# The first FFN product of six blocks by Strassen's algorithm in a fused attention and FFN kernel

## The chip, the cores and the metric

The kernel runs on one core of a Trainium2 chip. The metric is the device time of one execution in microseconds (us), the median of several runs. Engines are named as the profile names them: PE (TensorE matmul), PEld (its weight loads), DVE (VectorE), ACT (ScalarE), POOL (GpSimd) and SP (SyncE, which here issues all DMAs). L12 is line 12 of the kernel's source.

## The reference

Attention without softmax over 8 batches, 8 heads, 576 tokens and head size 64 feeds a token mixing of rank 32 and an FFN of 512 to 2048 to 512. Everything is fp32.

```python
kv = np.einsum('bhsd,bhse->bhde', k, v)
out = np.einsum('bhsd,bhde->bhse', q, kv)
rms = np.sqrt(np.mean(out * out, axis=-1, keepdims=True) + 1e-06)
x = out / rms * g_norm          # heads side by side: (8, 576, 512)
xt = x.transpose(0, 2, 1)
h = xt @ U @ V
u = x + h.transpose(0, 2, 1)
ch = np.maximum(u @ w_ch1, 0.0) @ w_ch2
return u + ch
```

## The kernel before

The 8 x 576 = 4608 tokens form `NBLK` = 9 blocks of `BLK` = 512. Hidden size 2048 is cut into `NF` = 16 chunks f of 128, model size 512 into `ND` = 4 chunks d. Activations lie transposed, features on partitions. An fp32 value is kept as two fp32r halves, hi and lo, and one fp32 product is three fp32r matmuls: hi·hi, hi·lo and lo·hi. So one f of a block has 4 x 3 matmuls of 128x512 in `ffn1` (L372 to L374) and 4 x 3 in `ffn2` (L389). `relu` makes the split hidden chunk: `hh` on ACT (L381), `hl` on DVE (L382). The chunk h has one PSUM bank (`ps_h`), y has four (`ps_y`) in which all 16 f are accumulated, and other products share three (`pp`). In program order ffn1 of f stands ahead of ffn2 of f-1.

All weights stay on chip. They arrive as encoded 64-bit words (`raw`, two 512 KB DMAs for each f) and are decoded in block 0, two f ahead of their use: `decode` on ACT (L82) and DVE (L85, L86, L88, L90) into a `dec` tile of 128x1024, then `split`: ACT copies the hi part into `ws` (L95), POOL subtracts for the lo part (L96).

The tokens of the next batch are prepared beside the FFN. For each of four head pairs: `kv_step` (k^T v), `out_step`, `stats_step`, `mul_step` (RMS norm), `xsplit_step` (xh, xl), `turn_step` (a transpose on DVE, L293, and 16 small DMAs `ut<-xt`, L296), `t_step`, `t4_step` (rank 32) and `mix_step`, whose two adds (L366) complete the rows `ut32` of u; `split_cols` makes `uth` and `utl` from them (L329, L330). `prep_schedule` gives each step a position, two to each f; head pairs follow every `gap` positions (STEPS0 with gap 3 in block 0, STEPS with gap 6 later). `finish` adds u to y (DVE L400, POOL L401) in one of three `st` buffers and sends it out (L402).

The written order is only a start: the tile framework's list scheduler orders the instructions of each engine from its own timeline, and each engine then runs its list in order. All DMAs are in one list, SP's. Tiles of pools with one buffer (`xt`, `kv_sb`, `q_sb`, `tails`) or three (`st`) make a later writer wait for the last reader.

Of the kernel before, what the change touches and what calls it, by code (L numbers as in the profile page):

```python
# [47 lines left out]
def build(ctx: ExitStack, tc: tile.TileContext, kv_in, kvt0_in, kvt_in, q_in, uv_in, g_in, w_in, out):  # L48
# [327 lines left out]
    def relu(h, end=False):  # L376
        if end:
            hh, hl = [sc.tile([P, BLK], F32R, name=f"h{s}_end", tag=f"x{s}") for s in "hl"]
        else:
# [1 line left out]
        nc.scalar.activation(out=hh, in_=h, func=AF.Relu)  # L381
        nc.vector.scalar_tensor_tensor(out=hl, in0=h, scalar=0.0, in1=hh.bitcast(F32), op0=ALU.max, op1=ALU.subtract)  # L382
# [9 lines left out]
    def finish(y, j):  # L392
        uh, ul = ut.pop(j)
        for c, cols, acc in y:
            if j == NBLK - 1:
                o = ut32[c][:, S - BLK + cols.start:S - BLK + cols.stop]
                nc.vector.scalar_tensor_tensor(out=o, in0=o, scalar=g_sb, in1=acc, op0=ALU.mult, op1=ALU.add)
            else:
                o = st.tile([P, DM], F32, name="st")
                nc.vector.tensor_tensor(out=o, in0=acc, in1=uh[:, c, :].bitcast(F32), op=ALU.add)  # L400
                nc.gpsimd.tensor_tensor(out=o, in0=o, in1=ul[:, c, :].bitcast(F32), op=ALU.add)  # L401
            nc.sync.dma_start(out=out[j, c][:, cols], in_=o)  # L402

    def outputs(j):

        y = [(c, slice(0, BLK), ps_y.tile([P, BLK], F32, name="y")) for c in range(ND)]
        if j == NBLK - 1:
            c, _, acc = y.pop()
            y.append((c, slice(0, BLK // 2), acc[:, 0:BLK // 2]))
            y.append((c, slice(BLK // 2, BLK), ps_p.tile([P, BLK], F32, name="pp")[:, 0:BLK // 2]))  # L410
        return y
# [80 lines left out]
    def prep_schedule(b):  # L492

        todo = {}
        if 0 < b <= B:
            todo[1] = [lambda: [split_cols(b - 1, c, 1, nc.gpsimd) for c in range(ND)]]
        if b < B:
            for p in range(NPAIR):
                steps = STEPS0 if b == 1 else STEPS
                base = steps["gap"] * p  # L500

                def kv(p=p):
                    kv_step(b, p)
                    nxt = (b, p + 1) if p + 1 < NPAIR else (b + 1, 0)
                    if nxt[0] < B:
                        load_kv(*nxt)

                def o(p=p):
                    for what in (out_step, stats_step, mul_step, xsplit_step, turn_step):
                        what(b, p)  # L510
                    nxt = (b, p + 1) if p + 1 < NPAIR else (b + 1, 0)
                    if nxt[0] < B:
                        load_q(*nxt)

                def t(p=p):
                    t_step(b, p)
                    t4_step(b, p)
# [95 lines left out]
```

## Time and profile before

| | |
|---|---|
| median of 3 runs | 941.3 us (940.36 to 941.7) |
| profiled execution | 941.2 us; span 939.4 us |
| busy: PE, DVE, ACT, POOL | 913.4, 428.2, 237.6, 88.7 us |
| first ffn1 of block 0; first ffn1 of block 1 | 39.46 us; 159.8 us |
| first ffn1 of block 8 | 848.1 us |
| DMA over the span | 65.48 MB, mean 70 GB/s |

Busy times are sums over the span. Since stages have different limits, a stage is read from its own stretch: how much of it each engine was busy, and which wait ended last. The clock column gives the TensorE clock that was granted, 1.00 for full speed. A matmul's "mean ns" in the groups counts overlapping neighbours twice; the spacing in the chain of work is its cost.

### The profile page before, as it was taken

What the parts mean: (1) busy time and instruction counts of PE and PEld (TensorE: products, weight loads), DVE (VectorE), ACT (ScalarE), POOL (GpSimd) and SP (SyncE); (2) the same over time, 40 slices, a digit from 0 to 9 for tenths busy, and PEclk for the clock granted to TensorE, in tenths of its full rate; (3) what the DMA queues carried; (4) which work ended last, traced back from release to release, by engine and by line L of the source; (5) the groups of instructions that cost most, each with busy time, mean ns of one, the idle gap of its engine ahead of it and who ended that gap; (6) DMA issues with size and microseconds to landing.
All of it is one profiled execution on the core that took longest, in us unless ns stands there. A gap on an engine that the chain in (4) does not pass through costs nothing.

```text
span 939.4 us, 11992 instructions
## 1 busy us (share of the span) xinstructions
PE 913.4 (97%) x4550; PEld 763.3 (81%) x4550; DVE 428.2 (46%) x824; ACT 237.6 (25%) x483; POOL 88.7 (9%) x82
## 2 busy tenths in 40 slices
...
DMA packets 45034, 65.48 MB, mean 70 GB/s; under 512 B 9904, under 2 KB 28080, under 8 KB 44976
## 3 DMA queue, kind: packets, MB, share of 16 engines
...
q14 instruction: 22, 0.18, 0.1%
...
## 4 chain that ended last, share of the span: by engine, by line
PE 84%; DVE 13%; DMA 1%; issue 1%; SPq 0%; ACT 0%; POOL 0%; DVEq 0%; POOLq 0%
PE y L389 37%; PE h L372 13%; PE h L373 13%; PE h L374 13%; DVE dec L88 3%; PE pp L219 2%; PE pp L240 2%; DVE dec L90 2%; DVE dec L86 2%; PE pp L304 2%; DVE dec L85 1%; DVE hl L382 1%; DMA w1raw<-w_in 1%; PE pp L364 1%; PE pp L389 1%
## 5 line engine op out<-in xcount | busy, mean ns | idle before, releaser
L389 PE MATMUL y<-hh,ws 128*128 128x512 f32 (+1 forms) x1072 | 351.0, 394 | 0.1
L382 DVE SCALAR_TENSOR_TENSOR hl<-h,hh 128x512 fp32r<-128x512 f32 x142 | 97.8, 689 | 307.8 <-ACT hh L381 307.2
L389 PEld LDWEIGHTS y<-hh,ws 128*128 128x128 f32 x1072 | 194.3, 188 | 36.0 <-ACT hh L381 0.8
L372 PE MATMUL h<-uth,ws 128*128 128x512 f32 x536 | 212.5, 397 | 6.9 <-DVE hl L382 6.9
L373 PE MATMUL h<-utl,ws 128*128 128x512 f32 x536 | 210.1, 392 | 0.0
L374 PE MATMUL h<-uth,ws 128*128 128x512 f32 x536 | 209.9, 392 | 0.0
L389 PE MATMUL y<-hl,ws 128*128 128x512 f32 (+1 forms) x536 | 207.6, 387 | 0.0
L381 ACT ACTIVATE hh<-h 128x512 fp32r<-128x512 f32 x142 | 84.8, 597 | 409.2 <-PE h L374 409.1
L372 PEld LDWEIGHTS h<-uth,ws 128*128 128x128 f32 x536 | 101.4, 189 | 31.0 <-DVE hl L382 10.8
L374 PEld LDWEIGHTS h<-uth,ws 128*128 128x128 f32 x536 | 101.2, 189 | 21.9
L373 PEld LDWEIGHTS h<-utl,ws 128*128 128x128 f32 x536 | 101.4, 189 | 20.4
L389 PEld LDWEIGHTS y<-hl,ws 128*128 128x128 f32 x536 | 100.6, 188 | 20.5
L401 POOL TENSOR_TENSOR st<-st,utl 128x512 f32<-128x512 f32 x32 | 40.7, 1296 | 676.7 <-DVE st L400 673.6
L366 DVE TENSOR_TENSOR ut<-pp,ut 128x288 f32<-128x288 f32 x56 | 25.0, 456 | 53.6 <-DMA ut<-xt 39.0
L96 POOL TENSOR_TENSOR ws<-dec,ws 128x1024 fp32r<-128x1024 f32 x15 | 37.4, 2495 | 60.6 <-ACT ws L95 60.6
L400 DVE TENSOR_TENSOR st<-y,uth 128x512 f32<-128x512 f32 x32 | 21.2, 686 | 44.5 <-PE y L389 33.0
L329 ACT ACTIVATE uth<-ut,g_sb 128x448 fp32r<-128x448 f32 (+7 forms) x56 | 27.6, 530 | 48.0 <-DVE ut L366 33.6
L330 DVE SCALAR_TENSOR_TENSOR utl<-ut,g_sb,uth 128x448 fp32r<-128x448 f32 (+7 forms) x56 | 28.2, 534 | 14.7 <-ACT uth L329 10.9
L253 DVE TENSOR_REDUCE ss<-x 128x10 f32<-128x640 f32 x32 | 26.1, 814 | 19.0 <-ACT x L244 19.0
L219 PE MATMUL pp<-kv_sb 128*128 128x128 f32 x232 | 31.4, 275 | 0.5 <-DVE t L313 0.5
L219 PEld LDWEIGHTS pp<-kv_sb 128*128 128x128 f32 x232 | 29.3, 191 | 2.0 <-DVE t L313 0.9
L240 PE MATMUL pp<-kvb,q_sb 128*128 128x128 f32 x224 | 29.6, 274 | 0.0
...
## 6 DMA issues: line engine op xcount, KB each, us to landing
raw<-w_in SPq DMA_DIRECT2D x30, 512.0 KB, 10.2
kv_sb<-kv_in SPq DMA_DIRECT2D x29, 512.0 KB, 3.5
...
out<-st SPq DMA_DIRECT2D x32, 256.0 KB, 2.0
ut<-xt SPq DMA_DIRECT2D x224, 20.0 KB, 1.8
ut<-xt SPq DMA_DIRECT2D x224, 16.0 KB, 1.8
...
kvq<-kv_in SPq DMA_DIRECT2D x3, 512.0 KB, 7.7
```

Of the source, the lines that this page charges most:

```text
L88: nc.vector.scalar_tensor_tensor(out=bits, in0=high, scalar=0xC0000000, in1=bits, op0=ALU.bitwise_and, op1=ALU.bitwise_or)
L96: lo_eng.tensor_tensor(out=lo, in0=src, in1=hi.bitcast(F32), op=ALU.subtract)
L219: nc.tensor.matmul(pp[:, 0:P], lhsT=m[:, i * P:(i + 1) * P], rhs=m[:, MAIN + i * P:MAIN + (i + 1) * P], start=(i == 0 and b < NATIVE), sto ...
L240: nc.tensor.matmul(big[:, i * P:(i + 1) * P], lhsT=qt[:, TAIL + i * P:TAIL + (i + 1) * P], rhs=kb, start=True, stop=True)
L330: nc.vector.scalar_tensor_tensor(out=lo, in0=src, scalar=g_sb, in1=hi.bitcast(F32), op0=ALU.mult, op1=ALU.subtract)
L372: nc.tensor.matmul(h, lhsT=w1s[f][0][:, d, :], rhs=uh[:, d, :], start=(d == 0), stop=False)
L373: nc.tensor.matmul(h, lhsT=w1s[f][0][:, d, :], rhs=ul[:, d, :], start=False, stop=False)
L374: nc.tensor.matmul(h, lhsT=w1s[f][1][:, d, :], rhs=uh[:, d, :], start=False, stop=(d == ND - 1))
L381: nc.scalar.activation(out=hh, in_=h, func=AF.Relu)
L382: nc.vector.scalar_tensor_tensor(out=hl, in0=h, scalar=0.0, in1=hh.bitcast(F32), op0=ALU.max, op1=ALU.subtract)
L389: nc.tensor.matmul(acc, lhsT=w2s[f][w][:, c, :], rhs=h[:, cols], start=(f == 0 and w == 0 and h is hh), stop=(f == NF - 1 and w == 1))
L401: nc.gpsimd.tensor_tensor(out=o, in0=o, in1=ul[:, c, :].bitcast(F32), op=ALU.add)
```

## The change

Blocks 0 to 2 stay as they are. Blocks 3 to 8 are taken in three pairs. A pair's u (512 x 1024 tokens) and w1 are cut in halves both ways: d halves by block halves for u (B11, B12, B21, B22), f halves (n and n + 8) by d halves for w1 (A11 to A22). Winograd's form of Strassen's algorithm computes the four quarters of h from 7 products in place of 8. Each product is of a weight form (`FORMS`) with a form of u (`WITH`), each again split in hi and lo: 2 x 3 = 6 matmuls of 128x512 (L517).

- The weight forms: A11, A12 and A22 are parts of w1, S1 to S4 sums of parts. `forms_of_w(n)`, eight times, positions in block 1, makes S1 to S4 on DVE (two L217 of 128x512, four L223 and four L228 of 128x256) and ACT (L224) in `st` buffers, and copies all seven (256 KB each) and the w2 of two f (512 KB each) to DRAM (L204): 22.9 MB.
- For each pair 8 x 7 forms are read back into a ring of 8 buffers, 7 loads ahead (L502); the w2 of a group, four tiles of 512 KB, is read into one set of buffers (L509).
- `forms_of_u` makes the seven forms of u for a pair, twice (two chunks i): 7 casts on ACT (L474), 7 subtractions (L475) and 4 more (L479) on DVE, all 128x512. u of blocks 3 to 8 is kept as one fp32 tile `r` (named `uth` or `utl` in the profile) in place of `uth`, `utl`.
- A pair runs in 4 groups of two row pairs: 14 products, with sums and relus between them (`after`; adds L524, `hl` L445), then 8 y units (`y_unit`, L565), each 12 matmuls in one bank of `ps_y`. After a unit DVE adds the bank to r (L524), or in the last group to an `st` tile that goes out.
- The lo part of a weight is subtracted on DVE (L105) in place of POOL, in block 0 also that of u's columns; `relu`'s special ending goes.
- Preparation: batches 1 and 2 as before, batches 3 and 4 both in block 2 (STEPS2, gap 3), 5 and 6 in pair 1, 7 in pair 2.

```diff
+STEPS2 = dict(kv=1, out=2, t=5, mix=8, gap=3)
+NSTD = 3
+NG = 4
+NPP = NF // 2 // NG
+HALF = NF // 2
+RING = 8
+FORMS = ["A11", "A12", "S2", "S1", "S3", "S4", "A22"]
+WITH = ["B11", "B21", "T2", "T1", "T3", "B22", "T4"]
...
-        split(w[:, 0], w[:, 1], t, nc.gpsimd)
+        split(w[:, 0], w[:, 1], t, nc.vector)
...
+    def to_dram(name, src):
+        t = dram.tile([P, 2, src.shape[-1]], F32, name=name)
+        nc.sync.dma_start(out=t, in_=src.bitcast(F32))
+        return t
+
+    def forms_of_w(n):
+
+        lower, upper = whole["w1"][n], whole["w1"][n + HALF]
+        c = DM // 2
+        for name, src in (("A11", lower[:, :, 0:c]), ("A12", lower[:, :, c:]), ("A22", upper[:, :, c:])):
+            w1d[n, name] = to_dram(f"w{name}_{n}", src)
+        for f in (n, n + HALF):
+            w2d[f] = to_dram(f"w2_{f}", whole["w2"][f])
+        a = dec.tile([P, 2 * DM], F32, name="dec")
+        for k, w in enumerate((lower, upper)):
+            nc.vector.tensor_tensor(out=a[:, k * DM:(k + 1) * DM], in0=w[:, 0].bitcast(F32), in1=w[:, 1].bitcast(F32), op=ALU.add)
+        a11, a12, a21, a22 = (a[:, k * c:(k + 1) * c] for k in range(4))
+        ts = {}
+
+        def form(name, in0, in1, op):
+            t = ts[name] = st.tile([P, 2, c], F32R, name="st")
+            nc.vector.tensor_tensor(out=t[:, 1].bitcast(F32), in0=in0, in1=in1, op=op)
+            nc.scalar.copy(out=t[:, 0], in_=t[:, 1].bitcast(F32))
+
+        def low(name):
+            t = ts.pop(name)
+            nc.vector.tensor_tensor(out=t[:, 1], in0=t[:, 1].bitcast(F32), in1=t[:, 0].bitcast(F32), op=ALU.subtract)
+            w1d[n, name] = to_dram(f"w{name}_{n}", t)
+
+        form("S1", a21, a22, ALU.add)
+        form("S2", ts["S1"][:, 1].bitcast(F32), a11, ALU.subtract)
+        low("S1")
+        form("S4", a12, ts["S2"][:, 1].bitcast(F32), ALU.subtract)
+        low("S2")
+        form("S3", a11, a21, ALU.subtract)
+        low("S4")
+        low("S3")
...
+        if b + part >= NSTD:
+            nc.scalar.mul(out=r_of(b + part)[:, c, lo:lo + n], in_=src, mul=g_sb)
+            return
...
+    def forms_of_u(j, i):
+
+        fs = sb["u"]
+        ra, rb = r_of(j), r_of(j + 1)
+        b11, b12, b21, b22 = ra[:, i], rb[:, i], ra[:, 2 + i], rb[:, 2 + i]
+
+        def parts(name, src):
+            nc.scalar.copy(out=fs[name][:, 0, i], in_=src)
+            nc.vector.tensor_tensor(out=fs[name][:, 1, i], in0=src, in1=fs[name][:, 0, i].bitcast(F32), op=ALU.subtract)
+
+        def less(in0, in1):
+            t = st.tile([P, BLK], F32, name="st")
+            nc.vector.tensor_tensor(out=t, in0=in0, in1=in1, op=ALU.subtract)
+            return t
+
+        parts("B11", b11)
+        parts("B21", b21)
+        t1 = less(b12, b11)
+        t2 = less(b22, t1)
+        parts("T2", t2)
+        parts("T1", t1)
+        t4 = less(b21, t2)
+        parts("T4", t4)
+        parts("T3", less(b22, b12))
+        parts("B22", b22)
...
+        g, rest = divmod(k % (HALF * len(FORMS)), NPP * len(FORMS))
+        n, a = divmod(rest, NPP)
+        t = sb["ring"][k % RING]
+        nc.sync.dma_start(out=t.bitcast(F32), in_=w1d[g * NPP + a, FORMS[n]])
+        loaded[k] = t
...
+    def product(k, n, bank, first):
+
+        w = loaded.pop(k).rearrange("p s (i f) -> p s i f", i=2)
+        u = sb["u"][WITH[n]]
+        for i in range(2):
+            for s, t in ((0, 0), (0, 1), (1, 0)):
+                nc.tensor.matmul(bank, lhsT=w[:, s, i], rhs=u[:, t, i], start=(first and i == 0 and s == 0 and t == 0),
+                                 stop=(i == 1 and s == 1), skip_group_check=not first)
...
+        if name == "A11":
+            nc.scalar.copy(out=s[0], in_=x)
+        elif name == "A12":
+            add(s[0], y, s[0])
+            relu_to(*h_of(a, "11"), s[0])
+        elif name == "S2":
+            nc.scalar.copy(out=s[1], in_=x)
+        elif name == "S1":
+            nc.scalar.copy(out=s[2], in_=y)
+        elif name == "S3":
+            add(s[2], x, s[2])
+            relu_to(*h_of(a, "22"), s[2])
+        elif name == "S4":
+            add(s[1], y, s[1])
+            relu_to(*h_of(a, "12"), s[1])
+        else:
+            relu_to(*h_of(a, "21"), x)
...
+    def y_units(j, g):
+
+        last = g == NG - 1
+        for part, halves in ((1, ("22", "12")), (0, ("11", "21"))):
+            r = r_of(j + part)
+            for c in range(ND):
+                end = j + 2 == NBLK and last and part == 0 and c == ND - 1
+                for cols in ([slice(0, BLK // 2), slice(BLK // 2, BLK)] if end else [slice(0, BLK)]):
+                    yield part, halves, r, c, cols, last
+
+    def y_unit(j, part, halves, r, c, cols, last):
+        acc = ps_y.tile([P, BLK], F32, name="y")[:, cols]
+        todo = [(name, a) for name in halves for a in range(NPP)]
+        for m, (name, a) in enumerate(todo):
+            hh, hl = h_of(a, name)
+            w = sb["w2"][2 * a + (name[0] == "2")]
+            for n, (s, h) in enumerate(((0, hh), (0, hl), (1, hh))):
+                nc.tensor.matmul(acc, lhsT=w[:, s, c * P:(c + 1) * P], rhs=h[:, cols],
+                                 start=(m == 0 and n == 0), stop=(m == len(todo) - 1 and n == 2))
+        if last:
+            o = st.tile([P, DM], F32, name="st")[:, cols]
+            add(o, acc, r[:, c, cols])
+            nc.sync.dma_start(out=out[j + part, c][:, cols], in_=o)
+        else:
+            add(r[:, c, cols], acc, r[:, c, cols])
...
+        elif j == 1:
+            todo = {}
+            rest_of(todo, 1)
+            pair_tasks(todo, 2, STEPS, 0)
+            for n in range(HALF):
+                todo.setdefault(3 + 3 * n, []).append(lambda n=n: forms_of_w(n))
+        else:
+            todo = {}
+            rest_of(todo, 2)
+            pair_tasks(todo, 3, STEPS2, 0)
+            pair_tasks(todo, 4, STEPS2, 12)
+            todo.setdefault(6, []).append(lambda: sb_tiles("ring"))
+            todo.setdefault(7, []).append(lambda: [load_form(k) for k in range(4)])
+            todo.setdefault(18, []).append(lambda: sb_tiles("u"))
+            todo.setdefault(27, []).append(lambda: forms_of_u(NSTD, 0))
+            todo.setdefault(30, []).append(lambda: forms_of_u(NSTD, 1))
...
+    k = 0
+    for j in range(NSTD, NBLK, 2):
+        todo = {}
+        if j < NBLK - 2:
+            rest_of(todo, j + 1)
+            for m, b in enumerate(range(j + 2, min(j + 4, B))):
+                pair_tasks(todo, b, STEPS, 24 * m)
+        at = 0
+        for g in range(NG):
+            banks = {}
+            for n in range(len(FORMS)):
+                for w in todo.get(at, []):
+                    w()
+                at += 1
+                for a in range(NPP):
+                    early = j == NSTD and g == 0 and n == 0 and a == 0
+                    if n == 0:
+                        banks[a, 0] = ps_p.tile([P, BLK], F32, name="pp") if early else ps_y.tile([P, BLK], F32, name="y")
+                    elif n == 1:
+                        banks[a, 1] = ps_y.tile([P, BLK], F32, name="y")
+                    which = int(FORMS[n] in ("A12", "S1", "S4"))
+                    product(k, n, banks[a, which], FORMS[n] in ("A11", "A12", "S1"))
+                    if early:
+                        ffn2(y_prev, [hprev])
+                        finish(y_prev, NSTD - 1)
+                        sb_tiles("rest")
+                        sb_tiles("ring2")
+                        load_w2(0)
+                        for i in range(4, RING - 1):
+                            load_form(i)
+                    after(n, a, banks[a, 0], banks.get((a, 1)))
+                    load_form(k + RING - 1 if k else RING - 1)
+                    k += 1
+            if g == NG - 1 and j + 2 < NBLK:
+                for i in range(2):
+                    forms_of_u(j + 2, i)
+            for unit in y_units(j, g):
+                for w in todo.get(at, []):
+                    w()
+                at += 1
+                y_unit(j, *unit)
+            if not (g == NG - 1 and j + 2 == NBLK):
+                load_w2((g + 1) % NG)
```

Three places in the engines' lists. First DVE in block 0, where f is decoded. Before, `dec` takes one f after the other; the lo part is not in DVE's list:

```order
L85 TENSOR_SCALAR dec<-dec 128x1024
L86 TENSOR_SCALAR dec<-dec 128x1024
L88 SCALAR_TENSOR_TENSOR dec<-raw_186,dec 128x1024
L382 SCALAR_TENSOR_TENSOR hl<-h,hh 128x512
L90 SCALAR_TENSOR_TENSOR dec<-raw_186,dec 128x1024
L85 TENSOR_SCALAR dec<-dec 128x1024
```

And now (L94 to L99 are the decode, L105 the lo part):

```order
L445 SCALAR_TENSOR_TENSOR hl<-h,hh 128x512
L94 TENSOR_SCALAR dec<-dec 128x1024 x2
L95 TENSOR_SCALAR dec<-dec 128x1024 x2
L97 SCALAR_TENSOR_TENSOR dec<-raw_188,dec 128x1024
L97 SCALAR_TENSOR_TENSOR dec<-raw_191,dec 128x1024
L445 SCALAR_TENSOR_TENSOR hl<-h,hh 128x512
L99 SCALAR_TENSOR_TENSOR dec<-raw_188,dec 128x1024
L99 SCALAR_TENSOR_TENSOR dec<-raw_191,dec 128x1024
L105 TENSOR_TENSOR ws_903<-dec,ws_903 128x1024
L105 TENSOR_TENSOR ws_1006<-dec,ws_1006 128x1024
L445 SCALAR_TENSOR_TENSOR hl<-h,hh 128x512
```

Two f are decoded side by side, one operation for both and then the next, and two subtractions of 128x1024 are added to them.

Second, DVE at the end of block 0 (the last three `hl` of block 0, with batch 1's last transpose `xt<-x` and the adds into `ut` of the head pairs). Before:

```order
L293 STREAM_TRANSPOSE xt<-x 128x5x4x32
L115 TENSOR_TENSOR xl<-x,xh 128x512
L281 TENSOR_TENSOR xh<-x,xh 64x128
L382 SCALAR_TENSOR_TENSOR hl<-h,hh 128x512
L366 TENSOR_TENSOR ut_1_90<-pp,ut_1_90 128x288 x2
L313 TENSOR_TENSOR t_1034<-pp,t_1034 32x128
L330 SCALAR_TENSOR_TENSOR utl<-ut_1_90,g_sb,uth 128x448
L382 SCALAR_TENSOR_TENSOR hl<-h,hh 128x512
L366 TENSOR_TENSOR ut_2_91<-pp,ut_2_91 128x288 x2
L313 TENSOR_TENSOR t_1106<-pp,t_1106 32x128
L330 SCALAR_TENSOR_TENSOR utl<-ut_2_91,g_sb,uth 128x448
L382 SCALAR_TENSOR_TENSOR hl<-h,hh 128x512
```

Now, from the last `hl` of block 0 on:

```order
L445 SCALAR_TENSOR_TENSOR hl<-h,hh 128x512
L350 STREAM_TRANSPOSE xt<-x 128x5x4x32
L124 TENSOR_TENSOR xl<-x,xh 128x512
L338 TENSOR_TENSOR xh<-x,xh 64x128
L272 TENSOR_TENSOR tails<-kvt_sb,tails 64x128
L273 TENSOR_TENSOR tails<-kvt_sb,tails 128x128
L426 TENSOR_TENSOR ut_1_92<-pp,ut_1_92 128x288 x2
L370 TENSOR_TENSOR t_1036<-pp,t_1036 32x128
L458 TENSOR_TENSOR st<-y,uth 128x512
L390 SCALAR_TENSOR_TENSOR utl<-ut_1_92,g_sb,uth 128x448
L458 TENSOR_TENSOR st<-y,uth 128x512 x2
L426 TENSOR_TENSOR ut_2_93<-pp,ut_2_93 128x288 x2
```

The last head pair's transpose stood three `hl` earlier and now stands behind the last one, with the adds of head pairs 1 and 2; those of head pair 3 follow four rows later. (L445 is `hl`, L350 the transpose, L426 the add into `ut32`, L458 what L400 was.)

Third, the end of pair 1, of which the kernel before has nothing. PE, from the fourth y unit of the last group on (y_5414; L361 and L424 are t and mix of batch 6's last head pair, L274 to L299 kv and out of batch 7's first):

```order
L565 MATMUL y_5414<-hs1_3779,w2r1_3783 128x512 x3
L361 MATMUL pp_5263<-xh_5128,u2_97 64x128 x5
L361 MATMUL pp_5263<-xl_5129,u2_97 64x128 x4
L424 MATMUL pp_5277<-v4_98,t4_5273 128x288
L424 MATMUL pp_5280<-v4_98,t4_5273 128x288
L274 MATMUL pp_5521<-tails_5522 128x256
L276 MATMUL pp_5521<-kv_sb_5069 128x128 x4
L297 MATMUL pp_5559<-kvb0_100,q_sb_5151 128x128 x4
L299 MATMUL pp_5564<-kvb0_100,q_sb_5151 128x128
L274 MATMUL pp_5694<-tails_5695 128x256
L276 MATMUL pp_5694<-kv_sb_5533 128x128 x4
L565 MATMUL y_5430<-hs0_3778,w2r0_3782 128x512 x3
```

DVE there, up to the add of the first y unit (y_5366):

```order
L426 TENSOR_TENSOR ut32_3_94<-pp_5277,ut32_3_94 128x288
L479 TENSOR_TENSOR st_5350<-utl_4035,st_5348 128x512
L475 TENSOR_TENSOR uB22_3319<-utl_4035,uB22_3319 128x512
L479 TENSOR_TENSOR st_5356<-uth_3806,st_5350 128x512
L479 TENSOR_TENSOR st_5360<-utl_4035 128x512
L310 TENSOR_REDUCE ss_5568<-x_90 128x10
L475 TENSOR_TENSOR uT2_3316<-st_5350,uT2_3316 128x512
L475 TENSOR_TENSOR uT4_3320<-st_5356,uT4_3320 128x512
L475 TENSOR_TENSOR uT3_3318<-st_5360,uT3_3318 128x512
L312 RECIPROCAL r0_5569<-ta_5570 128x10
L426 TENSOR_TENSOR ut32_3_94<-pp_5280,ut32_3_94 128x288
L524 TENSOR_TENSOR st_5379<-y_5366,utl_2859 128x512
```

The bank of y_5430, the fifth unit, is that of y_5366, whose add into `st` now stands behind batch 6's last adds and the second half of pair 2's forms of u.

More of the change, by code (lines that the diff above doesn't have):

```diff
@@ L157, in build @@
     w_sb = {"w1": w1s, "w2": w2s}
+    whole = {"w1": {}, "w2": {}}
+    w1d, w2d = {}, {}
     def load_first(which):
@@ L177, in decode_first @@
         keep(which, 0, w[:, 0], w[:, 1])
+        whole[which][0] = w[:, :, :]
     def decode_w(f):
@@ L394, in finish @@
         for c, cols, acc in y:
[L395 to L401, printed above, removed]
+            o = st.tile([P, DM], F32, name="st")
@@ L402, in finish @@
+            nc.vector.tensor_tensor(out=o, in0=acc, in1=uh[:, c, :].bitcast(F32), op=ALU.add)
+            nc.gpsimd.tensor_tensor(out=o, in0=o, in1=ul[:, c, :].bitcast(F32), op=ALU.add)
             nc.sync.dma_start(out=out[j, c][:, cols], in_=o)
     def outputs(j):
[L406 to L410, printed above, removed]
@@ L411, in outputs @@
-        return y
+        return [(c, slice(0, BLK), ps_y.tile([P, BLK], F32, name="y")) for c in range(ND)]
+    sb = {}
+    def forms_of_u(j, i):
[19 more added lines that the diff above has]
+        parts("B22", b22)
@@ new lines, in build, with load_form, load_w2 @@
+    loaded = {}
+    def load_form(k):
+        if k >= (NBLK - NSTD) // 2 * HALF * len(FORMS):
+            return
+        g, rest = divmod(k % (HALF * len(FORMS)), NPP * len(FORMS))
[3 more added lines that the diff above has]
+        loaded[k] = t
+    def load_w2(g):
+        for a in range(NPP):
+            for half in (1, 0):
+                t = sb["w2"][2 * a + half]
+                nc.sync.dma_start(out=t.bitcast(F32), in_=w2d[g * NPP + a + half * HALF])
@@ L490, in build @@
             ffn1(hs[f], f, [d], 0)
-    def prep_schedule(b):
-        todo = {}
[L495 to L517, printed above, removed]
-                for at, what in (("kv", kv), ("out", o), ("t", t), ("mix", lambda p=p: mix_step(b, p))):
-                    todo.setdefault(base + steps[at], []).append(what)
-        return todo
```

91 lines of the change are left out of this document (72 added, 19 removed).

## The prediction

> **What bounds the kernel now.** I read the page first, then the busy time by stretches, the chain, the groups of VectorE (DVE) and GpSimd (POOL) in block 0, and the DMAs. The page's head, the line of TensorE (PE) and the chain by engine:
>
> ```profile
> span 939.4 us, 11992 instructions
> ...
> PE 913.4 (97%) x4550; PEld 763.3 (81%) x4550; DVE 428.2 (46%) x824; ACT 237.6 (25%) x483; POOL 88.7 (9%) x82
> ...
> PE 84%; DVE 13%; DMA 1%; issue 1%; SPq 0%; ACT 0%; POOL 0%; DVEq 0%; POOLq 0%
> ```
>
> 97% over the whole hides two regimes. Busy time by stretches (stretch, its length, then busy us of each engine, granted clock, DMA share, GB/s):
>
> ```profile
> 25.00:50.00 25.00, 19.63 (x109) 16.64 (x110) 23.25 (x36) 14.26 (x28) 8.72 (x7) 0.86 1.03 408
> 50.00:75.00 25.00, 21.37 (x89) 16.94 (x88) 24.85 (x30) 11.15 (x14) 9.15 (x4) 0.93 0.41 158
> 75.00:100.00 25.00, 22.66 (x115) 18.01 (x115) 24.70 (x22) 12.22 (x18) 8.40 (x4) 1.00 0.14 41
> 100.00:125.00 25.00, 20.79 (x94) 16.18 (x93) 24.90 (x32) 11.40 (x18) 10.00 (x4) 0.93 0.16 46
> ...
> 160.00:260.00 100.00, 100.00 (x522) 84.47 (x521) 47.74 (x111) 25.82 (x59) 5.17 (x4) 1.00 0.25 74
> ...
> 750.00:840.00 90.00, 90.00 (x399) 74.36 (x398) 16.99 (x25) 12.74 (x21) 5.08 (x4) 1.00 0.03 12
> ```
>
> From 50 to 125 us DVE is busy 24.7 to 24.9 of every 25 us and PE is not: DVE is the bound of block 0, which decodes the weights. From 160 us on PE has no gap and DVE is at most half busy. There a matmul left out is its own time saved, and any new wait of PE is lost time. The chain in the steady part gives the price of a matmul:
>
> ```profile
> 778.00 0.23 PE h L374
> 778.23 2.72 PE y L389 x12
> ```
>
> 2.72/12 = 226.7 ns for one 128x512 fp32r matmul.
>
> **A. Fewer matmuls.** Before: 9 blocks x 16 f x (12 + 12) = 3456. After: 3 blocks x 384 = 1152, and 3 pairs x 4 groups x (14 products x 6 + 8 y units x 12 = 180) = 2160; together 3312. 144 fewer x 226.7 ns = **-32.6 us**, all on PE and on the path. The preparation of a batch has the same matmuls as before.
>
> **B. Decode: the subtraction goes from POOL to DVE.** Groups from 25 to 160 us, the last POOL's:
>
> ```profile
> L88 DVE SCALAR_TENSOR_TENSOR dec<-raw,dec 128x1024 uint32<-128x1024 uint32 x15 | 28.9, 1929 | 0.2
> L90 DVE SCALAR_TENSOR_TENSOR dec<-raw,dec 128x1024 uint32<-128x1024 uint32 x15 | 20.2, 1346 | 0.1
> L86 DVE TENSOR_SCALAR dec<-dec 128x1024 uint32<-128x1024 uint32 x15 | 18.0, 1200 | 0.2
> L85 DVE TENSOR_SCALAR dec<-dec 128x1024 f32<-128x1024 f32 x15 | 11.5, 768 | 1.5 <-ACT dec L82 1.5
> ...
> L330 DVE SCALAR_TENSOR_TENSOR utl<-ut,g_sb,uth 128x448 fp32r<-128x448 f32 x4 | 3.9, 982 | 2.4 <-ACT uth L329 2.4
> ...
> L281 DVE TENSOR_TENSOR xh<-x,xh 64x128 fp32r<-64x128 f32 x5 | 3.5, 708 | 0.1
> ...
> L96 POOL TENSOR_TENSOR ws<-dec,ws 128x1024 fp32r<-128x1024 f32 x15 | 37.4, 2495 | 60.6 <-ACT ws L95 60.6
> ```
>
> The timeline shows why the same instruction has two lengths (start, duration; the POOL row is from the same stretch):
>
> ```profile
> 70.14 1.22 DVE L88 SCALAR_TENSOR_TENSOR dec<-raw,dec 128x1024 uint32<-128x1024 uint32 x1
> ...
> 73.25 0.69 DVE L86 TENSOR_SCALAR dec<-dec 128x1024 uint32<-128x1024 uint32 x1
> 73.98 3.30 DVE L88 SCALAR_TENSOR_TENSOR dec<-raw,dec 128x1024 uint32<-128x1024 uint32 x1
> ...
> 73.78 2.42 POOL L96 TENSOR_TENSOR ws<-dec,ws 128x1024 fp32r<-128x1024 f32 x1 [5.03 <-ACT ws L95]
> ```
>
> L88 takes 1.22 us alone and 3.30 beside L96. So the stretch that POOL puts on DVE is 28.9 - 15 x 1.22 = 10.6, L90 1.9, L86 18.0 - 15 x 0.69 = 7.7, L85 1.2, and L330 and L281 (0.68 and 0.285 later on) 1.2 and 2.1: about 25 us. In exchange 15 subtractions of 128x1024 come onto DVE, at L88's undisturbed 1.22 us = 18.3, and the first four L217 (2.8). Net about -4 us of DVE; the order also puts two mix steps and the last transpose (some 4 us) behind the block's last `hl`. I take **-8 us** for the end of block 0. It can't gain more than its gap to PE's own work: block 0 takes 120.3 us (first ffn1 39.5, block 1 at 159.8) and PE has about 100 in it; ends -16 and 0.
>
> [...]
>
> **C0. Seam of blocks 0 and 1.** Before, the transpose of batch 1's last head pair ran well ahead of block 0's last `hl` (rows of DVE; then SP's queue, which issues its 16 transfers):
>
> ```profile
> 143.82 0.85 DVE L293 STREAM_TRANSPOSE xt<-x 128x640 f32<-128x640 f32 x1
> ...
> 156.60 0.69 DVE L382 SCALAR_TENSOR_TENSOR hl<-h,hh 128x512 fp32r<-128x512 f32 x1 [2.84 <-ACT hh L381]
> ...
> 165.68 0.69 DVE L382 SCALAR_TENSOR_TENSOR hl<-h,hh 128x512 fp32r<-128x512 f32 x1 [1.30 <-ACT hh L381]
> ...
> 144.69 10.01 SPq L296 DMA_DIRECT2D ut<-xt  x16
> ```
>
> In the new order the transpose stands behind that `hl`, so its chain is open when PE wants the fourth d chunk of block 1: 0.85 + 10.0 of issue + 1.8 to land (row below) + two adds 0.8 + split 0.7 + last three matmuls 0.7 + relu 0.6 = 15.5 us to the next `hl`, where 9.1 lay between the two before. **+6 us** (0 if the queue is early, 9 with a clock dip: 0.93 in a 25 us stretch is 1.75 us lost, and stretches with waits of PE show it).
>
> Groups of the steady part and DMA landings (KB each, median us from issue to landing), for what follows:
>
> ```profile
> L382 DVE SCALAR_TENSOR_TENSOR hl<-h,hh 128x512 fp32r<-128x512 f32 x112 | 77.3, 690 | 238.9 <-ACT hh L381 238.3
> L366 DVE TENSOR_TENSOR ut<-pp,ut 128x288 f32<-128x288 f32 x48 | 21.6, 457 | 53.1 <-DMA ut<-xt 39.0 <-PE pp L364 11.2 <-issue 2.8
> ...
> L253 DVE TENSOR_REDUCE ss<-x 128x10 f32<-128x640 f32 x24 | 19.6, 817 | 19.0 <-ACT x L244 19.0
> ...
> L115 DVE TENSOR_TENSOR xl<-x,xh 128x512 fp32r<-128x512 f32 x24 | 16.5, 688 | 0.0
> ```
>
> ```profile
> raw<-w_in SPq DMA_DIRECT2D x30, 512.0 KB, 10.2
> kv_sb<-kv_in SPq DMA_DIRECT2D x29, 512.0 KB, 3.5
> ...
> out<-st SPq DMA_DIRECT2D x32, 256.0 KB, 2.0
> ut<-xt SPq DMA_DIRECT2D x224, 20.0 KB, 1.8
> ```
>
> **C. Weight forms in block 1.** New on DVE: 12 L217 left x 0.69 and 64 adds of 128x256, not shown before; between 0.29 (L281's 64x128) and 0.457 (128x288) I take 0.41, near the latter. 8.3 + 26.2 = 34.5, so DVE goes from 47.7 to 82 of 100 us: not the bound, but `hl` stands behind more. Each form holds one of three st buffers until its 256 KB are written; at 2.0 us (out<-st, same size and direction) that is 32/3 x (about 3.6 of making and issue + 2.0) = 60 us of the block's 100. **+4 us** (0 to 15). The copies of A11, A12, A22 and w2 hold nothing; SP has them in block 0, behind the decode that the turns behind them wait for anyway.
>
> **D. Block 2 prepares two batches.** A preparation costs DVE about 28 us (47.7 per 100 us against 17.0 per 90). 17 + 56 + 22 forms of u x 0.69 = 88 of about 113 us: **+2** (0 to 5).
>
> **E. Block 2 to pair 1.** Behind the last `hl` DVE has 13 ops of L475/L479 (0.69, as L115), two L426, t4 and kvb: 10.7 us before T2's second half; PE has about 6.3 of work: **+5** with the next bank's wait (0 to 9).
>
> **F. Pair 1 to pair 2.** The fifth y unit needs the bank of the first, whose add stands behind t4, tails, kvb, two L426, seven L479/L475 and a reduce (0.8): about 10.3 us from the t matmuls on, with 4.2 us of PE's work in it; +1 for the relus ahead and 1.7 for a dip: **+9** (3 to 13). Pair 2 to 3 has no such steps in between: 0.
>
> [...]
>
> **G. In the groups.** Adds of y into r (0.69 per 2.72 us unit, four banks) and relus lie beside PE: +1 (0 to 4). Form loads come 7 products ahead, 7 x 1.36 = 9.5 us, of 256 KB, where kv_sb's 512 KB take 3.5: bandwidth is no limit (5.8 MB per 41 us group against the 408 GB/s shown). But SP issues in order, and one turn holds it 10.0 us, over the 9.5: a load behind it is up to 10.0 + 2.0 - 9.5 = 2.5 us late. Most of the 12 turns of the pairs fall in y units (21.8 of 41 us), where nothing is wanted: **+4** for the ring (0 to 16). The w2 loads have a whole product phase (19 us).
>
> **Sum:** -32.6 - 8 + 6 + 4 + 2 + 5 + 9 + 1 + 4 = -9.6. The profiled execution took 941.2 us (span 939.4), the median of the runs is 941.3: **932 us**.
>
> **Rivals.**
> 1. *The seams are covered.* Before, DVE waits 39.0 us in all for turns and PE shows no gap for it; if C0, E, F and the ring cost a few us together: 941.3 - 32.6 - 8 + 9 = 910. For it speaks the slack from 160 us on; against it, the orders, in which the adds stand behind the rest.
> [...]
> 3. *Block 0 gains nothing*, since DVE still has a row of decode for every f and PE waits for other work: B is 0, 940.
> 4. *SP is too slow for ring and turns.* If 6 to 12 turns land in product phases, 15 to 30 in place of 4: 943 to 958.
> 5. *Slower: the form writes hold DVE in block 1.* With a landing of 10.2 us (raw's row) each buffer is held 13.8 us, 32/3 x 13.8 = 147 us, so block 1 grows by 47: 975. It decides from a landing of 100 x 3/32 - 3.6 = 5.8 us. Against it, out<-st's 2.0; for it, that writes stand behind 10 us turns on SP and 14 MB of copies precede them.
>
> **Chances.** Forecast 0.44, with its own range 922 to 941; rival 1 0.18, 2 0.06, 3 0.08, 4 0.12, 5 0.12. Under 0.2% (1.9 us, about what a measurement of this kernel tells from no change) lie a little of the forecast and half of rival 3. Faster 0.43 + 0.18 + 0.06 + 0.04 = 0.71, same 0.05, slower 0.24. The range leaves out rival 5, the top of 4 and the lowest of 1: 908 to 955.
>
> **What would show it.** A: the product and y lines with 3312 matmuls at 0.227 in the chain. B: the decode lines at 1.22 and 0.69, and PE over 23 of 25 us from 50 to 125. C0, E, F: gaps of PE of 4 to 9 us at three seams, released by DVE. C: PE near 100% in block 1, and L223 waiting little for DMA. G: PE's waits for ring loads. Wrong I am if the gaps are missing (910), or if block 1 or the products wait for DMA (over 941).

## The result, and the profile after

931.15 us median (930.08 to 932.66, 4 runs) against 941.5 us: a ratio of 0.9893 (95% interval 0.9875 to 0.9911). The forecast was 932. The sum came out right, but by luck in part: its term for block 0 and its term for the seam behind block 0 were each off by some 6 us, in opposite directions. The profiled execution took 931.88 us. The page's head, PE's line and its granted clock in 40 slices:

```profile
span 930.1 us, 12741 instructions
...
PE 893.1 (96%) x4370; PEld 745.6 (80%) x4370; DVE 562.4 (60%) x1089; ACT 313.4 (34%) x629; POOL 23.5 (3%) x43
...
PEclk9799998999999999799999998999999999999999
```

PE is busy 20 us less, not 32.6: the new dips of the clock lengthen its matmuls, and its idle time grew from 26 to 37 us. Where, the stretches show (columns as before):

```profile
50.00:75.00 25.00, 23.00 (x100) 18.71 (x99) 23.22 (x32) 12.39 (x17) 0.00 (x0) 0.93 0.96 369
75.00:100.00 25.00, 25.00 (x127) 20.91 (x126) 23.79 (x31) 12.42 (x19) 0.00 (x0) 1.00 0.74 254
100.00:125.00 25.00, 25.00 (x126) 20.91 (x125) 23.85 (x37) 11.81 (x17) 0.00 (x0) 1.00 0.43 144
...
150.00:175.00 25.00, 19.08 (x82) 14.36 (x83) 14.14 (x35) 6.88 (x16) 3.25 (x3) 0.80 0.39 129
...
375.00:400.00 25.00, 20.21 (x92) 16.58 (x91) 18.90 (x40) 12.57 (x26) 5.27 (x4) 0.80 0.63 203
...
500.00:550.00 50.00, 47.12 (x234) 39.20 (x233) 31.22 (x64) 17.55 (x37) 0.00 (x0) 0.97 0.54 181
550.00:600.00 50.00, 43.04 (x204) 35.86 (x203) 29.52 (x62) 17.38 (x35) 0.00 (x0) 0.93 0.52 177
...
750.00:800.00 50.00, 50.00 (x222) 41.40 (x221) 17.70 (x27) 8.50 (x14) 0.00 (x0) 1.00 0.47 158
```

Block 0 is cured: PE fills it from 75 us on. Three seams lose time: blocks 0 to 1 (150 to 175), block 2 to pair 1 (375 to 400) and the last half of pair 1 (500 to 600). Each is idle time plus a slow clock. A clock of 0.80 over 25 us looks like another 5 us, but part of the slow time is idle time too, and that must not be counted twice. The first slow spell, in the same columns:

```profile
157.00:167.00 10.00, 7.42 (x15) 4.60 (x16) 8.63 (x22) 4.14 (x11) 1.65 (x1) 0.50 0.52 174
```

At half clock (the matmuls of 128x512 start 0.43 us apart from 164.69 to 166.83, and 0.23 apart from 167.18 on) about half of PE's busy time is lost: some 3.7 us here. Taken in steps of 0.25 us (busy time times what the clock lacks to 1.00), the loss is:

| stretch of the changed kernel | PE idle | lost to the clock |
|---|---|---|
| 150 to 175 | 5.9 | 3.8 |
| 375 to 400 | 4.8 | 3.8 |
| 540 to 552 | 2.9 | 1.4 |
| 564 to 582 | 7.0 | 2.6 |

By the same working the clock costs 19.8 us over the whole span, where it cost 6.6 in the kernel before.

Pair 3 runs without a gap. Its chain:

```profile
722.65 19.04 PE y L517 x84
741.70 21.76 PE y L565 x96
```

(19.04 + 21.76)/180 = 226.7 ns for each matmul, as before, so the 144 that are gone are worth the full 32.6 us.

DVE's `hl` mark the stages. The last `hl` of block 0 was at 156.60 us and is at 142.31; the first of block 1 was at 165.68 and is at 162.93. The first of block 2 was at 267.48 and is at 266.29. The rest of the span shrank from 671.9 to 663.8 us.

### The profile page after: what moved, and what is told of

Its sections match the earlier page's. It is cut to its first block, busy times and chain, and to the rows that moved or that the text cites. A ratio compares the mean times of both kernels' runs of the same rounds, so it can differ in the third digit from the quotient of the medians.

```text
span 930.1 us, 12741 instructions
## 1 busy us (share of the span) xinstructions
PE 893.1 (96%) x4370; PEld 745.6 (80%) x4370; DVE 562.4 (60%) x1089; ACT 313.4 (34%) x629; POOL 23.5 (3%) x43
## 4 chain that ended last, share of the span: by engine, by line
PE 78%; DVE 7%; DMA 7%; SPq 5%; issue 2%; ACT 1%; DVEq 0%; ACTq 0%
PE y L565 28%; PE y L517 22%; PE y L451 8%; SPq L353 4%; PE h L434 3%; PE h L435 3%; PE h L436 3%; PE pp L276 2%; PE pp L297 2%; DMA wS<-st 2%; DMA ringw<-wS 2%; PE pp L361 1%; DMA w2r<-w 1%; DVE st L223 1%; DMA ut<-xt 1%
## 5 line engine op out<-in xcount | busy, mean ns | idle before, releaser
L565 PE MATMUL y<-hs,w2r 128*128 128x512 f32 (+1 forms) x1164 | 271.5, 390 | 0.0
L565 PEld LDWEIGHTS y<-hs,w2r 128*128 128x128 f32 x1164 | 216.4, 189 | 43.6
L451 PE MATMUL y<-hh,ws 128*128 128x512 f32 x360 | 118.1, 397 | 0.0
L434 PE MATMUL h<-uth,ws 128*128 128x512 f32 x180 | 72.4, 402 | 3.6 <-DVE hl L445 3.6
L451 PEld LDWEIGHTS y<-hh,ws 128*128 128x128 f32 x360 | 65.6, 188 | 12.7 <-ACT hh L444 0.4
L436 PE MATMUL h<-uth,ws 128*128 128x512 f32 x180 | 71.7, 398 | 0.0
L435 PE MATMUL h<-utl,ws 128*128 128x512 f32 x180 | 71.5, 397 | 0.0
L451 PE MATMUL y<-hl,ws 128*128 128x512 f32 x180 | 70.5, 392 | 0.0
L517 PE MATMUL y<-uT,ringw 128*128 128x512 f32 x282 | 68.9, 392 | 0.0
L517 PE MATMUL y<-uT,ring 128*128 128x512 f32 x276 | 67.2, 392 | 0.0
L524 DVE TENSOR_TENSOR uth<-y,uth 128x512 f32<-128x512 f32 x36 | 24.9, 691 | 65.5 <-PE y L565 65.5
L517 PEld LDWEIGHTS y<-uT,ringw 128*128 128x128 f32 x282 | 52.3, 188 | 10.5
L517 PEld LDWEIGHTS y<-uT,ring 128*128 128x128 f32 x276 | 51.3, 188 | 10.6
L517 PE MATMUL y<-uB,ring 128*128 128x512 f32 x216 | 53.9, 399 | 2.8 <-DMA ring<-wS 2.8
L517 PE MATMUL y<-uB,ringw 128*128 128x512 f32 x210 | 53.2, 399 | 0.0
L524 DVE TENSOR_TENSOR sums<-y,sums 128x512 f32<-128x512 f32 x48 | 33.1, 690 | 32.3 <-PE y L517 27.0
L445 DVE SCALAR_TENSOR_TENSOR hl<-h,hh 128x512 fp32r<-128x512 f32 x47 | 32.3, 687 | 33.0 <-ACT hh L444 32.9
L517 PEld LDWEIGHTS y<-uB,ring 128*128 128x128 f32 x216 | 41.3, 192 | 11.5 <-issue 3.0
L524 DVE TENSOR_TENSOR utl<-y,utl 128x512 f32<-128x512 f32 x36 | 24.7, 689 | 38.1 <-PE y L565 37.8
L517 PEld LDWEIGHTS y<-uB,ringw 128*128 128x128 f32 x210 | 39.9, 192 | 8.1
```

Of the source, the lines that this page charges most:

```text
L434: nc.tensor.matmul(h, lhsT=w1s[f][0][:, d, :], rhs=uh[:, d, :], start=(d == 0), stop=False)
L435: nc.tensor.matmul(h, lhsT=w1s[f][0][:, d, :], rhs=ul[:, d, :], start=False, stop=False)
L436: nc.tensor.matmul(h, lhsT=w1s[f][1][:, d, :], rhs=uh[:, d, :], start=False, stop=(d == ND - 1))
L451: nc.tensor.matmul(acc, lhsT=w2s[f][w][:, c, :], rhs=h[:, cols], start=(f == 0 and w == 0 and h is hh), stop=(f == NF - 1 and w == 1))
L517: nc.tensor.matmul(bank, lhsT=w[:, s, i], rhs=u[:, t, i], start=(first and i == 0 and s == 0 and t == 0), stop=(i == 1 and s == 1), skip_g ...
L524: nc.vector.tensor_tensor(out=out, in0=in0, in1=in1, op=ALU.add)
```

## The experiments

Each edit is against the changed kernel unless it says otherwise. Ratios are to the kernel before on the same chip.

**The subtraction back on POOL.**

```diff
-        split(w[:, 0], w[:, 1], t, nc.vector)
+        split(w[:, 0], w[:, 1], t, nc.gpsimd)
```

> The changed kernel with one part undone: the lo part of the decoded weights is subtracted on POOL again (15 subtractions of 128x1024). Theory (POOL beside DVE stretches the decode, and moving the subtraction is what shortens block 0): L97 goes from 1.22 back to about 1.9 us and L95 to about 1.2 us in the mean, block 0's last hl from 142.3 to 152-157 us. The kernel's time then rises by 5 to 12 us, to 936-943 us, less than block 0 loses if the seam behind it has more cover. Rival (the new order of the decode, two f side by side, shortened block 0): last hl within 2 us of 142.3, time within 2 us of 931.

946.67 us, ratio 1.0049 (1.0037 to 1.0062): 15.5 us more than the changed kernel, and slower than the kernel before. The last `hl` of block 0 is at 160.50 us. The decode's groups from 25 to 160 us, of the changed kernel:

```profile
L105 DVE TENSOR_TENSOR ws<-dec,ws 128x1024 fp32r<-128x1024 f32 x15 | 18.2, 1221 | 1.7 <-ACT ws L104 1.6
...
L97 DVE SCALAR_TENSOR_TENSOR dec<-raw,dec 128x1024 uint32<-128x1024 uint32 x15 | 18.0, 1214 | 0.0
```

and with the subtraction on POOL:

```profile
L97 DVE SCALAR_TENSOR_TENSOR dec<-raw,dec 128x1024 uint32<-128x1024 uint32 x15 | 31.7, 2113 | 0.2
```

L97 stretches from 1214 to 2113 ns with POOL's subtraction beside it. The theory's direction holds, but the loss is above its range (5 to 12 us), and the last `hl` is later than its 152 to 157. DVE is busy 123.7 us from 25 us to the end of that `hl`, against 109.2. The decode is not where these 14.5 us lie: its four lines take 75.9 us here, and with L105 its five lines take 74.7 us in the changed kernel, so the stretch cost about what the subtractions cost. The small operations beside it weigh more. L313 of the norm takes 0.16 us in the changed kernel; here one that met a subtraction (DVE's row, then POOL's) ended with it:

```profile
107.32 2.33 DVE L313 TENSOR_TENSOR ta<-r 128x10 f32<-128x10 f32 x1
```

```profile
106.80 2.83 POOL L105 TENSOR_TENSOR ws<-dec,ws 128x1024 fp32r<-128x1024 f32 x1 [4.10 <-ACT ws L104]
```

With L315, L338 and the small L105 of u's columns this comes to 9.4 us from 25 to 160 us. Together with L97, L95 and L94, DVE's operations are some 28 us longer beside POOL's 38 us of subtractions. The last transpose also stands ahead of that `hl` in this list; how the rest divides was not separated.

**The subtraction on DVE, in the kernel before, alone.** The diff above the other way round, on the kernel before; nothing of Strassen.

> The kernel before with this part of the change alone: the lo part of the decoded weights on DVE. Theory: block 0's last hl goes from 156.6 to 143-149 us, and since the kernel before has its last transpose three hl ahead of the block's end, most of it stays: 941.5 becomes 929-936 us, so about as good as the whole change. Rival (the subtractions cost DVE what the collisions cost it, 18 against 25 us, and PE is bound elsewhere): 938-942 us.

933.7 us, ratio 0.9922 (0.9898 to 0.9946). The last `hl` of block 0 is at 143.01 us, 13.6 earlier, of the 14.3 that the whole change brings there. The next `hl` follows 15.2 us later, where it was 9.1, so part of this is lost again at the seam. So this one line does nearly all that the whole change does: 0.9922 and 0.9893 have overlapping intervals, and the seven products show some 2.6 us of their 32.6, which the intervals don't tell from none.

**Reads of forms and of w2 on a queue of their own.**

```diff
-        nc.sync.dma_start(out=t.bitcast(F32), in_=w1d[g * NPP + a, FORMS[n]])
+        nc.gpsimd.dma_start(out=t.bitcast(F32), in_=w1d[g * NPP + a, FORMS[n]])
...
-                nc.sync.dma_start(out=t.bitcast(F32), in_=w2d[g * NPP + a + half * HALF])
+                nc.gpsimd.dma_start(out=t.bitcast(F32), in_=w2d[g * NPP + a + half * HALF])
```

> The changed kernel with the reads of weight forms and of w2 issued by POOL's queue, which is empty in the pairs, in place of SP's. Theory (a turn holds SP 10 to 13 us and ring loads wait behind it): PE's waits for ring loads at the start of pair 1 and in its fourth group (1.9 + 2.8 us and the half clock after them) go, 931 becomes 922-927 us; the wait of 5.2 us at the end of pair 1 stays. Rival (the loads are late because they land slowly, 4.3 us at the median, with w2's 512 KB ahead of them): waits of the same size, 929-933 us, or more if POOL issues more slowly than SP.

922.53 us, ratio 0.9796 (0.9777 to 0.9816): 8.6 us gained. In the changed kernel SP's queue at the start of pair 1 reads:

```profile
367.41 13.02 SPq L353 DMA_DIRECT2D ut<-xt  x16
380.53 1.95 SPq L502 DMA_DIRECT2D ring<-wS  x4
```

The reads for the third form stand behind a turn's 16 transfers, and PE gets the first of them at 383.51:

```profile
383.51 2.90 PE L517 MATMUL pp<-uT,ring 128*128 128x512 f32 x6 [1.93 <-DMA ring<-wS]
```

The same happens at 546.57, where PE waits 2.8 us: a turn held SP from 531.34 to 543.52. PE's waits in the changed kernel (total us, times, longest):

```profile
PE pp L274 <- DVE ut L426: 8.2, 3, 5.2
...
PE y L517 <- DMA ring<-wS: 2.8, 1, 2.8
...
PE pp L517 <- DMA ring<-wS: 1.9, 1, 1.9
```

With POOL's queue no wait for a ring load is left in that list, and 500 to 550 us is full:

```profile
500.00:550.00 50.00, 50.00 (x254) 41.99 (x253) 34.04 (x69) 19.47 (x41) 9.64 (x18) 1.00 0.53 173
```

The wait for L426 at pair 1's end stays, as expected (8.0 us in all, 5.5 the longest). It is the queue, not the landing: ring<-wS lands 4.3 us after its issue at the median in both.

The time of issue is the larger part here: a turn's 16 transfers take 10 to 13 us to issue, and each of them, 16 or 20 KB, lands in 1.8 at the median.

**Batch 1's preparation closer together.**

```diff
-STEPS0 = dict(kv=1, out=2, t=6, mix=11, gap=3)
+STEPS0 = dict(kv=1, out=2, t=6, mix=8, gap=2)
```

> The changed kernel with batch 1's preparation, in block 0, at shorter distance: STEPS0 gap 2 in place of 3 and mix at 8 in place of 11. In the new list the last transpose stands one hl earlier, ahead of block 0's last. Theory (the seam of blocks 0 and 1 costs 11.5 us because this transpose and its 10 us of transfers start behind the last hl): the gap between block 0's last hl and block 1's first falls from 20.6 to 12-16 us and the time to 923-928 us. Rival (the seam is late for other reasons, or DVE's work in block 0 only moves the last hl back by as much): block 1's first hl within 2 us of 162.9, time 929-933 us.

925.01 us, ratio 0.9827 (0.9807 to 0.9847): 6.1 us gained. In the changed kernel DVE's timeline has the transpose behind the last `hl` of block 0, and the next `hl` 20.6 us later:

```profile
142.31 0.69 DVE L445 SCALAR_TENSOR_TENSOR hl<-h,hh 128x512 fp32r<-128x512 f32 x1 [0.44 <-ACT hh L444]
142.92 0.83 DVE L350 STREAM_TRANSPOSE xt<-x 128x640 f32<-128x640 f32 x1
...
162.93 0.69 DVE L445 SCALAR_TENSOR_TENSOR hl<-h,hh 128x512 fp32r<-128x512 f32 x1
```

Its transfers and the matmul that waits for them:

```profile
143.78 10.99 SPq L353 DMA_DIRECT2D ut<-xt  x16
```

```profile
157.23 0.80 PE L434 MATMUL h<-uth,w1s 128*128 128x512 f32 x1 [3.20 <-ACT uth L389]
```

With gap 2 the transpose is ahead of that `hl`, and the distance is 16.7 us:

```profile
137.30 0.84 DVE L350 STREAM_TRANSPOSE xt<-x 128x640 f32<-128x640 f32 x1 [0.15 <-DVE ut L426]
140.57 0.69 DVE L445 SCALAR_TENSOR_TENSOR hl<-h,hh 128x512 fp32r<-128x512 f32 x1 [1.87 <-ACT hh L444]
157.25 0.68 DVE L445 SCALAR_TENSOR_TENSOR hl<-h,hh 128x512 fp32r<-128x512 f32 x1
```

16.7 is just over the expected 12 to 16; the time is inside. What else stands in the 20.6 us, ACT's row first, then DVE's:

```profile
160.28 0.59 ACT L444 ACTIVATE hh<-h 128x512 fp32r<-128x512 f32 x1
```

```profile
160.86 0.83 DVE L350 STREAM_TRANSPOSE xt<-x 128x640 f32<-128x640 f32 x1
161.62 0.38 DVE L223 TENSOR_TENSOR st<-st,dec 128x256 f32<-128x256 f32 x1
```

`hh` is ready at 160.87, but `hl` runs at 162.93, behind the next batch's transpose and split and a form's sum. With gap 2 block 1's first `hl` comes 5.7 us earlier than in the changed kernel. Of the 11.5 us that the seam was longer than before, 7.6 remain.

**Batch 6's preparation earlier in pair 1.**

```diff
-                pair_tasks(todo, b, STEPS, 24 * m)
+                pair_tasks(todo, b, dict(STEPS, gap=5), 20 * m)
```

(Batch 7, in pair 2, gets gap 5 too.)

> The changed kernel with the preparations in pair 1 closer together: gap 5 in place of 6, batch 6 from position 20 in place of 24, so that batch 6's last mix stands 7 positions earlier and ahead of pair 1's last y units. Theory (the 5.2 us wait at pair 1's end, with the short waits around it and the half clock after them some 9 us, is the chain t4, mix adds, forms of u, first add of y on DVE): the wait goes and the time falls from 931 to 922-926 us. Rival (DVE has too much to do in pair 1, and the wait only moves to another group): a wait of 3 us or more elsewhere in pair 1, 929-933 us.

922.84 us, ratio 0.9805 (0.979 to 0.982): 8.3 us gained. The longest wait that goes is this one, on PE's timeline of the changed kernel:

```profile
574.87 0.55 PE L274 MATMUL pp<-tails 128*128 128x256 f32 x1 [5.16 <-DVE ut L426]
```

and the chain that leads to it is DVE's list, in order:

```profile
568.28 0.47 DVE ut L426
...
569.21 0.69 DVE st L479
569.90 0.65 DVE uB L475
570.55 1.20 DVE st L479 x2
571.75 0.73 DVE ss L310
572.49 0.41 DVE uT L475
...
573.60 0.68 DVE uT L475
...
574.41 0.32 DVE ut L426
```

The second add (L426) of a mix stands behind seven operations for the forms of u. It holds the PSUM bank that batch 7's kv (L274) wants, which stands ahead of the fifth y unit in PE's list. With the edit, 500 to 600 us has 98.0 us of PE in place of 90.2. But the edit moves turns as well: the wait for a ring load at 546.57 (2.8 us) is gone too, so the 8.3 us are not this chain's alone.

```profile
500.00:550.00 50.00, 49.40 (x246) 40.83 (x246) 36.12 (x73) 19.66 (x41) 0.00 (x0) 1.00 0.63 212
550.00:600.00 50.00, 48.64 (x238) 40.65 (x237) 31.30 (x64) 19.42 (x40) 0.00 (x0) 1.00 0.52 177
```

**The forms of u later instead.**

```diff
-                for i in range(2):
-                    forms_of_u(j + 2, i)
-            for unit in y_units(j, g):
+                forms_of_u(j + 2, 0)
+            for n, unit in enumerate(y_units(j, g)):
+                if n == 4 and g == NG - 1 and j + 2 < NBLK:
+                    forms_of_u(j + 2, 1)
```

> The changed kernel with the second half of pair 2's forms of u emitted after the fourth y unit of pair 1's last group, not ahead of the first; batch 6's mix stays where it is. If the forms of u on DVE ahead of the first add of y are what PE waits for at pair 1's end, the wait shrinks by their 5 us and the time falls to 923-927 us. Rival (batch 6's mix chain itself is what is late, or the forms are then late for pair 2's first products): 929-933 us, with a wait of PE before T2 or T1 of pair 2.

924.3 us, ratio 0.9826 (0.9811 to 0.9841): 6.9 us gained. The longest wait for L426 falls from 5.2 to 2.6 us. Here the wait for a ring load stays (2.9 us, at 548), so these 6.9 us are the chain's; idle time and clock from 500 to 600 us cost 7.4 us in place of 13.9. The forms of u between t and the last add are what cost the time.

**The three edits together**: form reads on POOL's queue, gap 2 in block 0, gap 5 in the pairs.

> The three edits together: ring and w2 reads on POOL's queue, batch 1's preparation at gap 2, pair 1's preparations at gap 5. If the seams are independent, their gains add: 931 - 8.6 - 6.1 - 5 to 9 = 907-912 us, without a wait of PE over 3 us from block 1 on except at block 0's end. Rival (they share one cause, DVE's list, and only the last one counts): 915-922 us.

906.09 us, ratio 0.9627 (0.9612 to 0.9641): the best version. 25.1 us less than the changed kernel, where the three alone gave 8.6 + 6.1 + 8.3 = 23.0, and just under the expected 907 to 912. The gains add up, though the first and the third each take away the wait at 546.57. PE's line and clock on its page:

```profile
PE 879.7 (97%) x4370; PEld 736.5 (81%) x4370; DVE 560.5 (62%) x1089; ACT 312.1 (35%) x629; POOL 138.7 (15%) x259
...
PEclk9799999999999999999999999999999999999999
```

PE is busy 13.4 us less than in the changed kernel with the same 4370 matmuls: that is mostly the granted clock, 0.991 over the span in place of 0.974. By the working above, 7.4 us are lost to it in place of 19.8.

**And the forms of u later on top.** The edits of the two versions above together.

> As the one with three edits, and the second half of pair 2's forms of u after the fourth y unit. If the forms still delay the first adds of y at pair 1's end there, 1 to 3 us less than with three edits; if they become late for pair 2's first products, up to 5 us more.

908.42 us, ratio 0.9646 (0.9628 to 0.9664): no gain over the three. Neither expectation is met clearly: the time is 2.3 us more, the two intervals overlap, and PE has no gap from 500 to 600 us, so the forms are not late for pair 2 there.

**The two edits of block 0 without Strassen.** The kernel before, with the subtraction on DVE and gap 2.

> The kernel before with the subtraction on DVE and batch 1's preparation at gap 2, nothing of Strassen: what the two edits are worth without it. Theory (Strassen's 144 matmuls are worth up to 32.6 us where the seams are closed, and block 0 is a matter of its own): 933.7 falls by 0 to 6 us, to 928-934, so that the version with three edits (906.1) is 22 to 28 us ahead of it. Rival (most of that version's gain comes from these two edits in block 0): 915-920 us.

930.01 us, ratio 0.9874 (0.9851 to 0.9898). The version with three edits is 23.9 us ahead of it: with the seams cut, the seven products, with all that the pairs need for them, bring 23.9 of their 32.6 us. The traces show where the other 8.7 went: from 142 us to the end PE idles 10.3 us and loses 1.6 to the clock with three edits, and here 2.6 and nothing.

**Batch 4 earlier, on top of the three edits.**

```diff
-            pair_tasks(todo, 4, STEPS2, 12)
+            pair_tasks(todo, 4, STEPS2, 10)
```

> The version with three edits (906.1 us) and batch 4's preparation in block 2 from position 10 in place of 12. What is left there of the seam of block 2 and pair 1 is 3.3 us of idle PE at 350-375 and a dip of the clock behind it. If batch 4's last steps and the forms of u behind them are late on DVE, 902-905 us; if DVE's work in block 2 (two preparations) is what fills the seam, 905-908 us.

914.13 us, ratio 0.9698 (0.9669 to 0.9728): 8 us worse, a miss for both expectations. DVE's timeline with three edits:

```profile
359.29 0.84 DVE L350 STREAM_TRANSPOSE xt<-x 128x640 f32<-128x640 f32 x1
```

and with batch 4 from position 10:

```profile
363.35 0.46 DVE L426 TENSOR_TENSOR ut<-pp,ut 128x288 f32<-128x288 f32 x1 [0.45 <-DMA ut<-xt]
363.72 0.68 DVE L445 SCALAR_TENSOR_TENSOR hl<-h,hh 128x512 fp32r<-128x512 f32 x1
...
371.27 0.83 DVE L350 STREAM_TRANSPOSE xt<-x 128x640 f32<-128x640 f32 x1
...
378.59 0.46 DVE L426 TENSOR_TENSOR ut<-pp,ut 128x288 f32<-128x288 f32 x1 [3.90 <-DMA ut<-xt]
```

Written two positions earlier, the last transpose ahead of pair 1 came 12 us later. The `x` that it turns comes at 369.88, behind eight operations for the first half of pair 1's forms of u; with three edits it stood ahead of them, at 358.38. PE's longest wait is for the `xh` made from this `x`, not for the turn:

```profile
369.88 0.68 DVE L322 TENSOR_TENSOR x<-pp,r 128x512 f32<-128x512 f32 x1
```

```profile
371.56 0.55 PE L361 MATMUL pp<-xh,u 128*64 128x128 f32 x4 [4.34 <-ACT xh L112]
```

Why the scheduler put it there is not known; a position is a wish, the list is what runs.

## Why the prediction was right, step by step

| step | forecast | measured |
|---|---|---|
| A, 144 matmuls | -32.6 | -32.6 (226.7 ns each in pair 3) |
| B, block 0 to its last `hl` | -8 (-16 to 0) | -14.3 |
| C0, seam of blocks 0 and 1 | +6 (0 to 9) | +11.5 (20.6 in place of 9.1) |
| C, block 1 | +4 (0 to 15) | +1.6 (103.4 in place of 101.8) |
| D to G, from block 2 on | +21 | +24.5 (-8.1 with A's -32.6) |
| sum | -9.6 | -9.3 |

The direction, the size and the three seams were forecast with their mechanisms. Two errors of some 6 us cancel in it, which is luck.

**B** was too small. The decode itself behaves as the rows said: L97 at 1214 ns, and the five lines with L105 take 74.7 us where four took 78.6, 3.9 less. But DVE's work up to the last `hl` fell by 12.3 us (from 25 us on 121.5 to 109.2). The terms of the forecast for work that moved behind this `hl` and for small stretched operations were together too low, and DVE's idle time in the stretch shrank by another 2. That the one line is the cause is shown: without Strassen it gives 13.6 of the 14.3 us.

**C0** was mis-sized at its end. Up to PE's release the chain was as described: 14.9 us from the `hl` to 157.23, where the forecast's terms give 14.2. From there to the next `hl` it had 1.3 us (three matmuls and a relu), and 5.7 were measured: 3.6 to the end of `hh`, with the clock at 0.50, and 2.1 in which `hl` stood behind other work in DVE's list.

**D to G** has the right sum with other parts. E (block 2 to pair 1) was put down to DVE's forms. The trace has 2.1 us of waiting there for a mix add and 1.9 for a ring load held by a turn on SP, and with 3.8 us of clock the seam costs 8.6, not 5: G's mechanism did about as much of it as E's. F was near: 9.6 us with the clock, for the forecast 9, and 6.9 come back where only the forms of u are moved; but the releaser was another, the PSUM bank of the next kv in place of y's. G's ring was +4 in the sum; the wait at 546.57 costs 4.3 with its clock, and moving the reads to another queue gave 8.6 in E and G together. D's block 2 shows next to nothing: 0.4 us of idle PE from its first `hl` to 374 us. Together 8.6 + 4.3 + 9.6 + 0.4 = 22.9 of the 24.5. The clock, which the forecast took at nothing to 1.75 us for a seam, cost 3.8 us in C0's, 3.8 in E's and 2.6 in F's.

**C** was lower, and hardly the forms' doing: block 1's first 4 us are still at half clock, and from 167 to 266 us PE idles 0.7 us. The writes land as out<-st suggested, and DVE's waits for st buffers come to 7.4 us in all:

```profile
wS<-st SPq DMA_DIRECT2D x32, 256.0 KB, 2.3
```

```profile
DVE st L223 <- DMA wS<-st: 7.4, 6, 2.4
```

So rival 5 (a landing over 5.8 us) fell by its own condition. Rival 1 (seams covered, 910) fell in the changed kernel; three edits made its number true. Rival 3 (block 0 gains nothing) fell with B. What POOL's subtraction costs DVE was priced nearly right: beside 38 us of it DVE's operations are some 28 us longer, for the forecast's 25. Rival 4 was present in small: PE waited twice for a ring load, not behind 6 to 12 turns.

What stays open: what fills the 16.7 us between block 0's last `hl` and block 1's first that remain with gap 2 (1.4 of them are other work ahead of `hl` in DVE's list: `hh` is ready at 155.82), and how much of B's excess is moved work and how much is small operations.
